# Linear attention into a PReLU feed-forward block on one core: new order of the first loads, whole output tiles in the second stage, and block 1 starting its own first output tile

## The chip, the cores and the metric

The kernel runs on one core of a Trainium2 chip. The metric is the device time of one execution in microseconds (us), lower is better. The kernels that are compared in one table row ran on the same chip as the executions of the kernel before that they are set against. "Span" is the time between the first and the last instruction that the profile shows; the device time is about 2.1 us longer.

## The reference, cut to what matters

```python
def _attn_ref(q, k, v, g_norm):                     # q, k, v: (8 batches, 8 heads, 576, 64)
    kv = np.einsum('bhsd,bhse->bhde', k, v)
    out = np.einsum('bhsd,bhde->bhse', q, kv)
    rms = np.sqrt(np.mean(out * out, axis=-1, keepdims=True) + 1e-06)
    return out / rms * g_norm

def _moe_ref(x, w_in, w_out, alpha):                # x: (4608, 512), w_in: (512, 2048), w_out: (2048, 512)
    h = x @ w_in
    g = np.maximum(h, 0.0) + alpha * np.minimum(h, 0.0)
    return g @ w_out
```

The attention output of all heads of a token is one row of x.

## The kernel before

The 4608 tokens are worked off in nine blocks of 512. In a block, 16 groups of 128 columns of h are made (four matmuls each), ScalarE takes the negative part (`m_sb`), VectorE combines both parts to `gt`, and four output tiles of 128 tokens need 16 matmuls each on `gt` and w_out. In the steady part TensorE alternates four matmuls of block w with four output matmuls of block w-1. The first two batches get their attention on TensorE in transposed form; later batches have rows that are transposed by DMA (`xm`).

The parts that the change touches:

```python
    for h0 in (0, HH):                       # batch 0, by half of the heads
        for nm in "qkv":
            load(0, nm, h0, h0 + HH)
    # ...
    def load_rest():
        for i in range(WQ):
            load_w_in(i)
        for nm in "kvq":
            zero_rest(stages[1][nm])
        load(1, "k")
        load_w_out(0)
        load(1, "q")
        load(1, "v")
        for i in range(1, WQ):
            load_w_out(i)
    # ... second stage: output matmuls of block 0 around the attention of batch 1
    LATER = 4
    def ahead(g0, g1, tiles=range(TPW)):
        for g in range(g0, g1):
            for a in tiles:
                if a < TPW - 1 or g < LATER:     # the fourth tile stops after group 4
                    y_mm(ys[a], 0, a, g)
    regroup(1, "k")
    ahead(0, 3)
    regroup(1, "q")
    step_t(1, 0, S_POOL)
    # ... three more step_t
    ahead(3, 4, range(2))
    step_kv(1, pool=S_POOL)
    # ...
    step_tail_ssq(0, S_POOL)                 # tail of batch 1: sum, Ln, Exp and norm
    ahead(15, NF)
    # ... blocks 1 to 8
    for w in range(1, NW):
        steps = phase_steps(w + 1)           # attention of the next batch, in steps
        for g in range(NF):
            a, part = divmod(g, TPW)
            parts = range(part * TPW, (part + 1) * TPW)
            if w == 1:                       # block 1: rest of block 0's fourth tile
                a, y = TPW - 1, ys[TPW - 1]
                parts = [LATER + g] if LATER + g < NF else []
            # ... begin of the step, m1_group(w, g), mid of the step,
            # y_mm for parts, end of the step
```

## Time and profile before

| | before |
|---|---|
| device time, median of 3 | 294.23 us (294.08 to 294.52) |
| span of the profiled run | 291.3 us (its device time: 293.46 us) |
| TensorE busy | 281.1 us, 96% of the span |
| TensorE's holes between the first output matmul and block 2, by starts | 1.29 us in the second stage, 1.23 us in block 1 (0.98 in the prediction) |

VectorE's timeline in block 1 of the kernel before (start, duration, instruction):

```profile
61.93 0.74 DVE L487 SCALAR_TENSOR_TENSOR gt<-m_sb,beta_sb,h_ps 128x512 f16<-128x512 f32 x1
...
63.19 0.74 DVE L487 SCALAR_TENSOR_TENSOR gt<-m_sb,beta_sb,h_ps 128x512 f16<-128x512 f32 x1
```

These are gt 7 and gt 8, 2.9 and 3.1 us behind their groups' matmuls. No output matmul waited for them, since block 1 then multiplied only gt of block 0.

The prediction says that this lag cost nothing. It overlooked a hole that the timeline hides in a merged line:

```profile
64.13 3.86 PE L478 MATMUL h_ps<-xt,w_in_sb 128*128 128x512 f16 x16
```

Sixteen matmuls 0.216 us apart, the last shown as 0.38 us, would take 3.62 us and not 3.86. The single records have the gap: 64.78 + 0.22 to 65.24, 0.25 us, ahead of group 13, and name VectorE's gt as what was waited for. Group 13 takes the bank of group 9 (the code gives banks out in fours), and gt 9 ended at 65.18.

### The profile page before, as it was taken

What the parts mean: (1) busy time and instruction counts of PE and PEld (TensorE: products, weight loads), DVE (VectorE), ACT (ScalarE), POOL (GpSimd) and SP (SyncE); (2) the same over time, 40 slices, a digit from 0 to 9 for tenths busy, and PEclk for the clock granted to TensorE, in tenths of its full rate; (3) what the DMA queues carried; (4) which work ended last, traced back from release to release, by engine and by line L of the source; (5) the groups of instructions that cost most, each with busy time, mean ns of one, the idle gap of its engine ahead of it and who ended that gap; (6) DMA issues with size and microseconds to landing.
All of it is one profiled execution on the core that took longest, in us unless ns stands there. A gap on an engine that the chain in (4) does not pass through costs nothing.

```text
span 291.3 us, 4287 instructions
## 1 busy us (share of the span) xinstructions
PE 281.1 (96%) x1551; PEld 137.8 (47%) x1551; DVE 168.8 (58%) x261; ACT 152.7 (52%) x297; POOL 100.2 (34%) x111
## 2 busy tenths in 40 slices
PE   5999999999999999999999999999999999999994
PEld 2454454544454454454445544554445444444443
DVE  4569847787667576448744764488448644444300
ACT  1459457584666565438644754476448544444210
POOL 8833410584448128424733373233003100000000
PEclk9999999999999999999999999999999999999999
DMA  7999999999899826991699189934212311222133
GB/s 89 182 206 203 200 206 198 196 202 175 134 155 184 167 42 94 204 203 30 104 206 208 34 125 184 187 49 90 46 36 56 81 36 41 47 47 47 39 72 72
DMA packets 66228, 35.54 MB, mean 122 GB/s; under 512 B 32784, under 2 KB 61728, under 8 KB 66208
## 3 DMA queue, kind: packets, MB, share of 16 engines
q0 software_dynamic: 29664, 18.35, 45.5%
q1 hardware_dynamic: 36384, 16.80, 28.3%
q8 instruction: 12, 0.20, 0.3%
q10 hardware_dynamic: 160, 0.13, 0.2%
q14 instruction: 8, 0.07, 0.1%
HBM read 36.71 MB, written 9.44 MB: 158 GB/s over the span
## 4 chain that ended last, share of the span: by engine, by line
PE 76%; DMA 17%; DVE 2%; POOL 2%; issue 1%; ACT 1%; POOLq 0%; DVEq 0%
PE y_ps L505 38%; PE h_ps L478 34%; DMA vst<-in_v_dram 7%; DMA w_in_sb<-in_moe_w_in_dram 5%; DMA w_out_sb<-in_moe_w_out_dram 4%; PE kv_ps L245 2%; PE otm_ps L397 2%; DVE gt L487 1%; DMA xm<-xrow 1%; POOL w_in_sb L165 1%; DVE xrow L430 1%; DVE ss L409 0%; POOL rg L421 0%; POOL qst L97 0%; POOL kst L97 0%
## 5 line engine op out<-in xcount | busy, mean ns | idle before, releaser
L487 DVE SCALAR_TENSOR_TENSOR gt<-m_sb,beta_sb,h_ps 128x512 f16<-128x512 f32 x144 | 105.6, 744 | 74.6 <-ACT m_sb L485 73.9
L485 ACT ACTIVATE m_sb<-h_ps 128x512 f32<-128x512 f32 x144 | 85.4, 597 | 87.3 <-PE h_ps L478 86.1
L505 PE MATMUL y_ps<-w_out_sb,gt 128*128 128x512 f16 (+1 forms) x528 | 128.8, 373 | 0.0
L478 PE MATMUL h_ps<-xm,w_in_sb 128*128 128x512 f16 x448 | 115.0, 379 | 0.2 <-DMA xm<-xrow 0.2
L505 PEld LDWEIGHTS <-gt 128*128 128x128 f16 x592 | 57.6, 98 | 64.6
L478 PEld LDWEIGHTS <-w_in_sb 128*128 128x128 f16 x584 | 55.7, 98 | 61.5 <-issue 1.7
L421 POOL TENSOR_TENSOR rg<-ss,g_all 128x512 f32<-128x512 f32 (+1 forms) x30 | 31.3, 1042 | 78.9 <-ACT ss L419 70.9
L478 PE MATMUL h_ps<-xt,w_in_sb 128*128 128x512 f16 (+1 forms) x136 | 30.6, 366 | 0.1
L515 ACT COPY y_sb<-y_ps 128x512 f32<-128x512 f32 (+1 forms) x32 | 18.4, 575 | 15.9 <-PE y_ps L505 15.9
L409 DVE TENSOR_REDUCE ss<-sqm_sb 128x8 f32<-128x512 f32 (+1 forms) x30 | 20.5, 683 | 10.5 <-ACT sqm_sb L403 10.5
L430 DVE TENSOR_TENSOR xrow<-otm_ps,rg 128x512 f16<-128x512 f32 (+1 forms) x30 | 20.5, 682 | 3.6 <-POOL rg L421 3.6
L403 ACT ACTIVATE sqm_sb<-otm_ps 128x512 f32<-128x512 f32 (+1 forms) x30 | 17.7, 591 | 6.3 <-PE otm_ps L397 6.3
L112 POOL COPY ksb<-kst 128x2560 f16<-128x2560 f16 x6 | 13.9, 2324 | 14.6 <-DMA kst<-in_k_dram 14.6
L112 POOL COPY qsb<-qst 128x2560 f16<-128x2560 f16 x5 | 11.6, 2316 | 10.0 <-issue 10.0
L397 PEld LDWEIGHTS <-qtm 128*128 128x128 f16 x120 | 9.2, 98 | 7.1 <-DMA qtm<-qsb 0.3
L204 PE MATMUL warm_ps<-warm,mask 128*128 128x512 f16 x25 | 8.5, 479 | 3.3 <-DVE eps_t L146 3.3
L397 PE MATMUL otm_ps<-kv_sb,qtm 128*128 128x128 f16 x120 | 11.6, 219 | 0.0
L245 PEld LDWEIGHTS <-ksb 128*128 128x128 f16 x160 | 9.4, 98 | 3.8 <-issue 1.5
L245 PE MATMUL kv_ps<-vst,ksb 128*128 128x128 f16 x160 | 10.4, 219 | 0.9 <-DMA vst<-in_v_dram 0.7
L416 ACT ACTIVATE ss<-ss,eps_t 128x8 f32<-128x8 f32 (+1 forms) x30 | 9.0, 301 | 3.2 <-DVE ss L409 2.9
L513 DVE COPY y_sb<-y_ps 128x256 f32<-128x256 f32 x1 | 0.4, 425 | 13.4 <-PE y_ps L505 13.4
L249 DVE TENSOR_TENSOR kv_sb<-kv_ps,mask 128x512 f16<-128x512 f32 (+1 forms) x9 | 5.6, 627 | 3.7 <-PE kv_ps L245 3.7
(76 smaller groups left out, 136.0 us busy)
## 6 DMA issues: line engine op xcount, KB each, us to landing
out_dram<-y_sb SPq DMA_DIRECT2D x70, 128.0 KB, 2.3
kst<-in_k_dram POOLq DMA_DIRECT2D x7, 320.0 KB, 8.5
qst<-in_q_dram POOLq DMA_DIRECT2D x7, 320.0 KB, 4.8
vst<-in_v_dram POOLq DMA_DIRECT2D x7, 320.0 KB, 10.6
w_in_sb<-in_moe_w_in_dram POOLq DMA_DIRECT2D x4, 512.0 KB, 10.2
w_out_sb<-in_moe_w_out_dram POOLq DMA_DIRECT2D x4, 512.0 KB, 15.0
kst<-in_k_dram POOLq DMA_DIRECT2D x7, 256.0 KB, 9.5
qst<-in_q_dram POOLq DMA_DIRECT2D x7, 256.0 KB, 6.6
```

Source lines behind the costliest of these rows:

```text
L112: (eng or nc.vector).tensor_copy(out=bufs[b % NBUF][nm][:, :, h0:h1, :].rearrange("p t h d -> p h t d"), in_=stages[b % NBUF][nm][:, h0:h1],)
L245: nc.tensor.matmul(out=kv_ps[:, j - j0, :], lhsT=ks(t), rhs=vs(t), start=(t == 0), stop=(t == NT - 1),)
L397: nc.tensor.matmul(out=ot_ps[:, 2 * j : 2 * j + 2, :], lhsT=qtms[b][:, t * NPAIR + j, :], rhs=kvs[b, j], start=True, stop=True,)
L403: nc.scalar.activation(out=sq[0:n], in_=ot_ps[0:n], func=AF.Square)
L409: nc.vector.tensor_reduce(out=ss[0:n], in_=sq[0:n], op=ALU.add, axis=mybir.AxisListType.X,)
L421: nc.gpsimd.tensor_tensor(out=rg[0:n], in0=ss[0:n].unsqueeze(2).to_broadcast([n, H, D]), in1=g_all[0:n].unsqueeze(1).to_broadcast([n, H, D ...
L430: nc.vector.tensor_mul(out=x[0:n], in0=ot_ps[0:n], in1=rg[0:n])
L478: nc.tensor.matmul(out=h_ps[:, cols], lhsT=w_in_blk(c, g), rhs=xt_of(w, c)[:, cols], start=(c == 0), stop=(c == NC - 1 and cols.stop == W),)
L485: nc.scalar.activation(out=m_sb[:], in_=h_ps[:], func=AF.Relu, scale=-1.0)
L487: nc.vector.scalar_tensor_tensor(out=gt[:], in0=m_sb[:], scalar=beta_sb[:, g : g + 1], in1=h_ps[:], op0=ALU.mult, op1=ALU.add,)
L505: nc.tensor.matmul(out=y[:], lhsT=gts[w, g][:, a * P : (a + 1) * P], rhs=w_out_blk(g)[:, cols], start=(g == 0), stop=(g == NF - 1),)
L515: nc.scalar.copy(out=y_sb[:, cols], in_=y[:])
```

## The change

The intent: (1) load q of batch 0 whole and first, so that all its transposes are out of the way while k and v land; (2) load half of w_out ahead of batch 1, so that more output matmuls can fill the time until q, k and v of batch 1 are there; (3) finish all four output tiles of block 0 in the second stage; (4) let block 1 begin its own first output tile, two groups behind the making of gt.

```diff
+    load(0, "q")
     for h0 in (0, HH):
-        for nm in "qkv":
+        for nm in "kv":
             load(0, nm, h0, h0 + HH)
@@ load_rest
-        load(1, "k")
         load_w_out(0)
-        load(1, "q")
-        load(1, "v")
-        for i in range(1, WQ):
+        load_w_out(1)
+        for nm in "kqv":
+            load(1, nm)
+        for i in range(2, WQ):
             load_w_out(i)
@@ opening: order on TensorE (cut: transposes of all heads first, fewer warm-up
@@ matmuls, two matmuls with w_in ahead of the sum of squares, groups 4 and 5 begun early)
@@ second stage (cut)
     ahead(0, 3)
     regroup(1, "q")
+    ahead(3, 6)
     step_t(1, 0, S_POOL)
...
-    step_ot(1, 0, O1)
-    step_ot(1, 1, H_POOL[0])
+    step_ot(1, 0, H_POOL[0])
+    step_ot(1, 1, O1)
...
+    ahead(10, 11)
+    step_ot(1, 3, H_POOL[0])
     norm(1, 1)
     ssq_mm(1, 2, S_POOL)
-    ahead(9, 12)
+    ahead(11, QW)
+    ahead(QW, NF, (0,))
     ssq_mm(1, 3, S_POOL)
...
@@ blocks
+    AHEAD = NF - 2
...
             if w == 1:
-                a, y = TPW - 1, ys[TPW - 1]
-                parts = [LATER + g] if LATER + g < NF else []
+                parts = [(0, g - NF + AHEAD)] if g >= NF - AHEAD else []
+            else:
+                n0 = AHEAD if w == 2 else 0
+                n1 = TPW * NF - n0
+                parts = [divmod(n0 + i, NF) for i in range(n1 * g // NF, n1 * (g + 1) // NF)]
...
+            if (w, g) == (1, 1):
+                step_tail_ssq(0, (ps_o, "o0"))
+            if (w, g) == (1, 3):
+                tail_norm(0)
             for f in end:
                 f()
```

The buffers of batch 1 are now zeroed at the start, and the norm of the tail is a function of its own, called after group 3 of block 1, just ahead of the end of that step, in which kv of batch 2 is made.

More of the change, by code (lines that the diff above doesn't have):

```diff
@@ L123, in regroup_batch @@
             regroup(b, nm, eng=nc.gpsimd)
-    for nm in "qkv":
-        zero_rest(stages[0][nm])
+    for st in stages:
+        for nm in "qkv":
+            zero_rest(st[nm])
     ident = const_p.tile([P, P], FP32, name="ident")
@@ L130 @@
     HH = H // 2
+    load(0, "q")
     for h0 in (0, HH):
-        for nm in "qkv":
+        for nm in "kv":
             load(0, nm, h0, h0 + HH)
@@ L189, in load_rest @@
             load_w_in(i)
-        for nm in "kvq":
-            zero_rest(stages[1][nm])
-        load(1, "k")
         load_w_out(0)
-        load(1, "q")
-        load(1, "v")
-        for i in range(1, WQ):
+        load_w_out(1)
+        for nm in "kqv":
+            load(1, nm)
+        for i in range(2, WQ):
             load_w_out(i)
@@ L366, in step_tail_ssq, with tail_norm @@
         nc.scalar.activation(out=rstd[:], in_=rstd[:], func=AF.Exp, bias=0.0, scale=-0.5)
+        ots["tail", i] = (ot_ps, rstd)
+    def tail_norm(i):
+        ot_ps, rstd = ots.pop(("tail", i))
         nc.vector.scalar_tensor_tensor(
@@ L385, in transpose_q @@
         )
-    n_tile = [1]
+    n_tile = [2]
     def next_o():
@@ L540 @@
     keep_warm(10)
-    regroup(0, "q", 0, HH)
     nc.vector.tensor_scalar(
@@ L544 @@
     )
+    regroup(0, "q", 0, HH)
+    regroup(0, "q", HH, H)
     step_t(0, 0, H_POOL[0])
@@ L547 @@
     regroup(0, "k", 0, HH)
-    load_rest()
-    keep_warm(8)
-    step_kv(0, 0, 2)
-    keep_warm(2)
-    step_ot(0, 0)
-    step_ot(0, 1)
-    keep_warm(1)
-    regroup(0, "q", HH, H)
-    ssq_mm(0, 0)
     step_t(0, 2, H_POOL[2])
-    step_t(0, 3, H_POOL[0])
+    step_t(0, 3, (ps_o, "o0"), nc.scalar)
     alpha_ps = ps_h.tile([P, NF], FP32, name="alpha_ps", tag="h1")
@@ L568 @@
     )
-    ssq_mm(0, 1)
+    spread_g()
+    load_rest()
+    keep_warm(4)
+    step_kv(0, 0, 2)
+    keep_warm(2)
+    step_ot(0, 0)
+    step_ot(0, 1)
     regroup(0, "k", HH, H)
-    spread_g()
+    keep_warm(2)
+    ssq_mm(0, 0)
+    ssq_mm(0, 1, H_POOL[2])
+    step_kv(0, 2, 4)
     norm(0, 0)
-    keep_warm(2)
-    step_kv(0, 2, 4)
-    keep_warm(2)
+    keep_warm(3)
     load_batch(2)
@@ L581 @@
     first += [ps_o.tile([P, W], FP32, name="h_ps", tag=f"o{g}") for g in range(2)]
+    m1_mm(first[0], 0, 0, (0,))
+    m1_mm(first[1], 0, 1, (0,))
     half_ssq(0, O2)
+    m1_mm(first[2], 0, 2, (0,))
+    m1_mm(first[3], 0, 3, (0,))
     for g in range(4):
-        m1_mm(first[g], 0, g, (0,))
-    for g in range(4):
-        if g == 2:
-            half_ssq(1, O2)
         m1_mm(first[g], 0, g, (1,))
+    half_ssq(1, O2)
+    m1_mm(first[4], 0, 4, (0, 1))
     for i in range(2):
@@ L595 @@
         if i == 0:
-            m1_mm(first[4], 0, 4, (0, 1))
-    m1_mm(first[4], 0, 4, (2, 3))
-    m1_evac(first[4], 0, 4)
-    others = {5: (ps_s, "s"), 6: (ps_y, "y"), 7: O2, 11: (ps_o, "o0"), 12: (ps_o, "o1"),
+            first.append(ps_s.tile([P, W], FP32, name="h_ps", tag="s"))
+            m1_mm(first[5], 0, 5, (0, 1))
+    for g in (4, 5):
+        m1_mm(first[g], 0, g, (2, 3))
+        m1_evac(first[g], 0, g)
+    others = {6: (ps_y, "y"), 7: O2, 11: (ps_o, "o0"), 12: (ps_o, "o1"),
               13: (ps_s, "s")}
-    for g in range(5, NF):
+    for g in range(6, NF):
         m1_group(0, g, others.get(g))
-    LATER = 4
     ys = [
@@ L616, in ahead @@
             for a in tiles:
-                if a < TPW - 1 or g < LATER:
-                    y_mm(ys[a], 0, a, g)
+                y_mm(ys[a], 0, a, g)
     S_POOL = (ps_s, "s")
     O1 = (ps_o, "o1")
+    QW = NF - GW
     regroup(1, "k")
@@ L628 @@
     step_t(1, 3, H_POOL[1], nc.scalar)
-    ahead(3, 4, range(2))
+    ahead(6, 7)
     step_kv(1, pool=S_POOL)
-    ahead(3, 4, range(2, TPW))
-    step_ot(1, 0, O1)
-    step_ot(1, 1, H_POOL[0])
+    ahead(7, 8)
+    step_ot(1, 0, H_POOL[0])
+    step_ot(1, 1, O1)
     step_ot(1, 2, H_POOL[1], nc.vector)
-    ahead(4, 5)
+    ahead(8, 9)
     ssq_mm(1, 0, S_POOL)
-    ahead(5, 7)
+    ahead(9, 10)
     ssq_mm(1, 1, S_POOL)
     norm(1, 0)
-    ahead(7, 9)
-    step_ot(1, 3, O1, nc.vector)
+    ahead(10, 11)
+    step_ot(1, 3, H_POOL[0])
     norm(1, 1)
     ssq_mm(1, 2, S_POOL)
-    ahead(9, 12)
+    ahead(11, QW)
+    ahead(QW, NF, (0,))
     ssq_mm(1, 3, S_POOL)
@@ L648 @@
     transpose_q(2)
-    ahead(12, 13)
-    step_tail_ot(0, H_POOL[1])
-    ahead(13, 15)
+    y_out(ys[0], 0, 0)
+    ahead(QW, NF, (1,))
     norm(1, 3)
-    step_tail_ssq(0, S_POOL)
-    ahead(15, NF)
-    for a in range(TPW - 1):
-        y_out(ys[a], 0, a, nc.vector if a == 1 else None)
+    step_tail_ot(0, O1)
+    ahead(QW, NF, (2,))
+    y_out(ys[1], 0, 1, nc.vector)
+    y_out(ys[2], 0, 2)
+    ahead(QW, NF, (3,))
+    y_out(ys[3], 0, 3)
     LOAD_G = 6
-    n_group[0] = 0
+    n_group[0] = 1
+    AHEAD = NF - 2
     for w in range(1, NW):
@@ L667 @@
                 load_batch(w + 2)
-            a, part = divmod(g, TPW)
-            parts = range(part * TPW, (part + 1) * TPW)
             if w == 1:
-                a, y = TPW - 1, ys[TPW - 1]
-                parts = [LATER + g] if LATER + g < NF else []
+                parts = [(0, g - NF + AHEAD)] if g >= NF - AHEAD else []
[3 more added lines that the diff above has]
+                parts = [divmod(n0 + i, NF) for i in range(n1 * g // NF, n1 * (g + 1) // NF)]
             begin, mid, end = steps.pop(0) if steps else ([], [], [])
@@ L675 @@
                 f()
-            m1_group(w, g, [H_POOL[0], S_POOL, H_POOL[2], H_POOL[1]][g % 4] if w == 1 else None)
+            m1_group(w, g, [H_POOL[1], S_POOL, H_POOL[2], H_POOL[0]][g % 4] if w == 1 else None)
             for f in mid:
                 f()
-            if 0 in parts:
-                pool, tag = ((ps_y, "y"), (ps_s, "s"))[a % 2]
-                y = pool.tile([P, W], FP32, name="y_ps", tag=tag)
-            for gg in parts:
-                y_mm(y, w - 1, a, gg)
-            if NF - 1 in parts:
-                y_out(y, w - 1, a)
+            for a, gg in parts:
+                if gg == 0:
+                    pool, tag = ((ps_y, "y"), (ps_s, "s"))[a % 2]
+                    y = pool.tile([P, W], FP32, name="y_ps", tag=tag)
+                wy = w if w == 1 else w - 1
+                y_mm(y, wy, a, gg)
+                if gg == NF - 1:
+                    y_out(y, wy, a)
+            if (w, g) == (1, 1):
+                step_tail_ssq(0, (ps_o, "o0"))
+            if (w, g) == (1, 3):
+                tail_norm(0)
             for f in end:
```

## The prediction

> **What bounds the kernel now.** I read the busy table first, then busy time by stage, then TensorE's timeline. The first fence is the busy table; the second is busy time by stretch (start:end, length, then busy us and count of PE, weight loads, DVE, ACT, POOL, then clock, DMA share, GB/s). I cut the stretches where the first matmul with w_in, the first output matmul, block 1 and block 2 begin.
>
> ```profile
> PE 281.1 (96%) x1551; PEld 137.8 (47%) x1551; DVE 168.8 (58%) x261; ACT 152.7 (52%) x297; POOL 100.2 (34%) x111
> ```
>
> ```profile
> 17.43:31.86 14.43, 14.37 (x75) 7.13 (x74) 11.83 (x21) 11.27 (x19) 4.43 (x7) 1.00 1.30 203
> 31.86:48.80 16.94, 16.13 (x110) 8.31 (x109) 10.85 (x16) 9.07 (x15) 4.27 (x6) 1.00 1.33 202
> 48.80:68.22 19.42, 18.68 (x110) 9.04 (x108) 15.83 (x25) 13.80 (x30) 10.67 (x11) 1.00 1.22 192
> 68.22:287.25 219.03, 219.01 (x1184) 106.98 (x1184) 120.35 (x173) 112.49 (x226) 66.72 (x63) 1.00 0.60 103
> ```
>
> TensorE is the bound, and from 68.22 us on it has no hole (219.01 of 219.03 us). The change cannot gain there. What remains is the opening before 17.43 us, 0.81 us idle in the second stage and 0.74 us in block 1. The timeline of TensorE names the holes (start, duration, instruction, idle before it and releaser):
>
> ```profile
> 10.25 0.72 PE L245 MATMUL kv_ps<-vst,ksb 128*128 128x128 f16 x10 [0.30 <-DMA vst<-in_v_dram]
> ...
> 17.21 0.38 PE L327 MATMUL ssq_ps<-sq_sb,mask 128*128 128x512 f16 x1 [0.47 <-ACT sq_sb L267]
> ...
> 34.97 1.29 PE L221 MATMUL qt_ps<-ident,qsb 128*128 128x128 f16 x20 [0.35 <-DVE qsb L112]
> ...
> 38.88 0.80 PE L278 MATMUL ot_ps<-qt_sb,kv_sb 128*128 128x448 f16 x5 [0.33 <-DVE kv_sb L249]
> ...
> 53.71 1.28 PE L245 MATMUL kv_ps<-vst,ksb 128*128 128x128 f16 x20 [0.43 <-DMA vst<-in_v_dram]
> ...
> 68.22 1.02 PE L478 MATMUL h_ps<-xm,w_in_sb 128*128 128x512 f16 x4 [0.23 <-DMA xm<-xrow]
> ```
>
> A matmul of 512 columns is shown as 0.38 us, but the next starts 0.216 us after it; so I measure a hole from the last start plus 0.216. The second stage then loses 0.52 us (34.23+0.22 to 34.97, transposes wait for q's regroup), 0.28 (36.31+0.22 to 36.81) and 0.49 (to 38.88, kv_sb): **1.29 us**. Block 1 loses 0.58 us before kv of batch 2 (52.91+0.22 to 53.71; v had landed at 39.45+14.1) and 0.4 before block 2 (its transposed rows arrive last): **0.98 us**. That is all that reordering after 17.43 us can win, 0.8% of the time.
>
> **What the Trainium skill says.** "TensorE: Matmul & The Clock Gate", section "Wait — 56ns, not 53.3ns?", gives 215.7 ns start to start at N=512 when warm; the trace agrees (32.07, 32.29, 32.51). So a moved matmul costs 0.216 us wherever it goes. "PSUM — Partial Sum Buffer", section "PSUM: the matmul accumulator": 8 banks, and one matmul's output fits one bank. The code names exactly eight tags (h0-h2, o0-o2, s, y), each used for tiles of up to one bank. Four held by output tiles leave four to rotate, so when a bank comes free matters. "DMA: Bandwidth & Descriptors", section "Anatomy of one DMA — SWDGE (gpsimd) path", fits 2.0 us plus bytes over 436 GB/s. That would be 3.2 us for w_out's 512 KB pieces; here they take 15.0 us from issue to landing, behind one another, at about 200 GB/s. I therefore go by landing times, not by the fit.
>
> **The change part by part.**
>
> *q whole and first.* Landing times (issue plus latency) before: half q 5.7 us, half k 7.6, half v 10.1, second halves 11.6, 13.1, 14.7, first w_in 17.2, second 19.7. The order becomes q, q, k, v, k, v. The same number of bytes precede the end of v and w_in, so these still land at 14.7 and 17.2; the first half of v moves to about 11.4. DVE also zeroes three more buffers first (3 x 0.27 = 0.8 us), so the warm-up matmuls start near 4.0, not 3.25; q's wait hides that. kv of heads' first half moves from 10.25 to about 11.6, and ACT's Square, Ln, Exp chain, which ended at 15.56, to about 16.8. The Square of the other half then begins at 16.8 instead of 16.57, in time for 17.4. TensorE meanwhile puts two matmuls on w_in ahead of that sum of squares, hiding the 0.47 us, but w_in lands only at 17.2, so they begin where the sum began. Following both orders on, the first four groups finish at 22.4 us in either. The early rate is 162 GB/s against 206 later; fewer, larger q loads may lift it a little. I allow **-0.2 us**, an estimate.
>
> *Half of w_out ahead of batch 1.* w_out 0 and 1 land near 28.7 and 31.3, batch 1 about 2.5 to 5 us later: k 33.9, q 36.3, v 39.1 (v ended at 36.6, followed by w_out 1 at 39.1; the same bytes). The last half of w_out and batch 2 keep their times (41.7, 44.9, 53.5).
>
> *Second stage.* 24 output matmuls (24 x 0.216 = 5.2 us) fill 31.87 to 37.05. q lands at 36.3, its regroup takes 0.83, so transposes start at 37.2: a hole of 0.15. Next kv starts near 39.25, as v lands; four matmuls (0.86) cover most of kv_sb, which took from 36.81 to 38.82, so 2.0 us with kv's own 1.1. Later, output tile 3 of attention asks for bank h0. The norm that frees it ended 42.71 when its sum of squares began at 40.16: 2.55 us. TensorE reaches that place ten matmuls later, 2.16 us: a hole of about 0.45. So 1.29 becomes 0.6: **-0.69 us**.
>
> *Four whole output tiles.* Twelve matmuls of the fourth tile move out of block 1 into the second stage; none is added: 0 us by themselves. Block 1 starts near 50.6 instead of 51.2 (48.80 + 12 x 0.216, less the tail's sum).
>
> *Block 1.* kv of batch 2 now comes near 54.7, after v's 53.5: the 0.58 goes. Transposed rows get as much extra time as work is put before them, so the 0.4 goes too: **-0.98 us**. But two new waits arise. First, the tail's Ln and Exp (0.69+0.63) now lie between ACT's second and third m_sb, and its norm (0.75 on DVE) lies just before kv_sb. ACT then gives m_sb 2 near 55.0; DVE works gt 2, gt 3, tail norm and kv_sb (0.7 each) to about 57.85. TensorE wants kv_sb at 56.9, after kv (1.12), a group (0.86) and an output matmul (0.22). In full 1.0 us; **+0.7** taken. Second, the output tile follows only two groups behind: gt must be ready 2.16 us after its group's matmuls. Around the first three tiles of batch 2 it was not: group 7's matmuls ended at 59.76 and its gt at 62.67, 2.9 us later, group 8's 3.1, group 9's 3.25. Before, this lag cost nothing because block 1 multiplied block 0's gt. At the full lag the waits sum to 1.0 to 1.3 us; **+0.8** taken. At the seam to block 2, gt 15 is also barely late: **+0.1**.
>
> **Sum:** -0.2 - 0.69 - 0.98 + 0.7 + 0.8 + 0.1 = -0.27 us; 294.23 - 0.27 = 293.96, so **294.0 us**.
>
> **The rivals.** (a) *The holes go and no new ones come.* ACT and DVE are 71% and 82% busy in block 1, so their lag might shrink once the arrival of kv is later and steadier. Then -0.2 - 0.69 - 0.98 gives 292.4. For it: the order looks tuned around these holes. Against it: gt's measured lag of 2.9 to 3.25 us. (b) *DVE and ACT become the bound of block 1.* Both new waits in full (1.0 + 1.3), and no gain in the opening: 294.23 - 0.69 - 0.98 + 2.3 + 0.1 = 295.0. For it: DVE's in-order queue with tail norm ahead of kv_sb. (c) *Transfers cap the second stage.* Loads already run without a gap at about 200 GB/s until 53 us. If q of batch 1 lands 1 us later than 36.3, all of it shows, since the 24 matmuls end at 37.05: about 295.0. Against it: the bytes ahead of it are known. (d) *The opening gains more.* If whole-q loads ran at 206 GB/s from the start, w_in would land some 0.5 us earlier and half a microsecond more would be saved.
>
> **Range and chances.** Rivals (a) and (b) span 292.4 to 295.0; I widen a little for rivals (c) and (d) and rounding of landing times: 292.4 to 295.4. A 2% change is 5.9 us. All post-opening holes sum to 2.3 us, so faster by 2% would need most of the opening's filler to vanish: 0.02. Slower by 2% needs a serialisation I have not seen: 0.02. Within 2%: 0.96.
>
> **What would show it right or wrong.** In the changed profile: first matmuls with w_in at about 17.2 us, and the step from h to output matmuls still near 31.9; transposes of batch 1 near 37.2 with a wait on q's regroup below 0.5 us; no DMA wait before kv of batch 2; a wait of the first otm_ps matmuls on kv_sb near 57 us; waits of output matmuls on gt in the second half of block 1; a stretch from block 2 on as dense as now. I am wrong if w_in lands clearly before 17 us (then faster), if gt keeps within 2.16 us of its group (then about 292.5), or if batch 1 arrives later than the output matmuls cover (then slower).

## More of the kernel before

The chain of work that ended last, by engine, on the page of the kernel before:

```profile
PE 76%; DMA 17%; DVE 2%; POOL 2%; issue 1%; ACT 1%; POOLq 0%; DVEq 0%
```

The 17% of DMA are, but for 1% of transposed rows, the loads of the first 54 us, one queue that from 4 us on moves 162 to 214 GB/s; the chain leaves it at the last load of batch 2's v.

## The result, and the profile after

The changed kernel takes 293.40 us (median of 4, 293.03 to 293.72) against 294.15 us (median of 4). The ratio is 0.9973 with a 95% interval of 0.9955 to 0.999: the same within 2%, and a small gain. Ratios in this text are from fast runs of the same rounds; they are not quite the ratio of the medians. They agree with the ratio of the means of all listed executions within 0.0002, but for two kernels whose first, profiled execution stands apart: whole q alone (0.9974, 0.9981 by all five) and loads as before (1.0149 and 1.0136). A second timing, on another chip, gives 0.9979 (0.9958 to 0.9999). There three of the kernel before's 11 executions took 295.0 to 295.5 us and lift its mean; by medians the gain is only 0.3 us (293.65 against 293.96).

The profile after: the busy table's first line and, below it, the chain of work that ended last.

```profile
PE 280.4 (96%) x1547; PEld 137.0 (47%) x1547; DVE 167.5 (57%) x258; ACT 153.6 (53%) x299; POOL 99.1 (34%) x109
...
PE 88%; ACT 3%; DVE 3%; DMA 2%; issue 1%; POOL 1%; DVEq 0%; POOLq 0%
```

The DMA queue has left the chain (17% to 2%): TensorE and the waits on ScalarE and VectorE carry it from the opening on.

Busy time by stretch (columns as in the prediction), cut at the same four places of the program as in the prediction (first matmul with w_in, first output matmul, block 1, block 2):

```profile
16.50:31.53 15.03, 14.77 (x74) 7.16 (x75) 12.78 (x21) 11.91 (x21) 4.22 (x6) 1.00 1.27 204
31.53:50.14 18.61, 18.40 (x121) 9.46 (x120) 10.60 (x16) 9.78 (x17) 4.78 (x7) 1.00 1.36 201
50.14:70.89 20.75, 19.52 (x113) 9.21 (x111) 15.58 (x24) 13.28 (x29) 10.98 (x12) 1.00 1.18 191
70.89:287.35 216.46, 216.20 (x1171) 105.51 (x1169) 120.31 (x173) 112.72 (x226) 65.87 (x62) 1.00 0.59 102
```

TensorE's idle time fell from 0.81 to 0.21 us in the second stage and rose from 0.74 to 1.23 us in block 1. From block 2 on it is dense as before, but for 0.26 us, most of which is the seam below. TensorE's timeline says who was waited for:

```profile
16.50 0.61 PE L482 MATMUL h_ps<-xt,w_in_sb 128*128 128x512 f16 x2 [0.29 <-DMA w_in_sb<-in_moe_w_in_dram]
...
36.71 1.28 PE L221 MATMUL qt_ps<-ident,qsb 128*128 128x128 f16 x20
...
44.94 0.39 PE L278 MATMUL ot_ps<-qt_sb,kv_sb 128*128 128x64 f16 x2 [0.21 <-DVE xt L305]
...
54.24 1.28 PE L245 MATMUL kv_ps<-vst,ksb 128*128 128x128 f16 x20
...
57.23 0.38 PE L401 MATMUL otm_ps<-kv_sb,qtm 128*128 128x128 f16 x4 [0.63 <-DVE kv_sb L249]
...
63.84 0.39 PE L509 MATMUL y_ps<-w_out_sb,gt 128*128 128x512 f16 x1 [0.60 <-DVE gt L491]
...
65.09 0.39 PE L509 MATMUL y_ps<-w_out_sb,gt 128*128 128x512 f16 x1
...
72.31 0.60 PE L509 MATMUL y_ps<-w_out_sb,gt 128*128 128x512 f16 x2 [0.18 <-DVE gt L491]
```

The transposes at 36.71 and kv of batch 2 at 54.24 no longer wait. The wait for the bank of the fourth attention tile (44.94), the wait on kv_sb (57.23), and the waits on gt (63.84 and the two that follow it, and 72.31) are new. As before, holes are measured from starts: 44.35 + 0.22 to 44.94 is 0.37 us; 56.22 + 0.22 to 57.23 is 0.79; 62.21 + 0.86 to 63.84 is 0.77, and the next two output matmuls come 0.17 and 0.16 late; 71.75 + 0.22 to 72.31 is 0.34. VectorE's timeline of the changed kernel shows what the 57.23 waited for:

```profile
54.42 1.41 DVE L491 SCALAR_TENSOR_TENSOR gt<-m_sb,beta_sb,h_ps 128x512 f16<-128x512 f32 x2 [0.97 <-ACT m_sb L489]
55.74 0.74 DVE L371 SCALAR_TENSOR_TENSOR xm<-ot_ps,g2col,rstd 128x512 f16<-128x512 f32 x1
56.41 0.68 DVE L249 TENSOR_TENSOR kv_sb<-kv_ps,mask 128x512 f16<-128x512 f32 x1
```

VectorE worked in the order of the program: gt 2 and 3, the tail's norm (L371), and only then kv_sb, although kv's matmuls had ended at 55.52.

At an equal place in block 3 (the output matmuls right after kv) the two first traces stand at 103.95 us before and 103.99 us after. So by this pair of traces the change moved time but won none, while the timed runs say 0.75 us. The experiments had to explain both.

### The profile page after: what moved, and what is told of

Same layout as the page of the kernel before. It is cut to its first block, busy times and chain, and to the rows that moved or that the text cites. A ratio compares the mean times of both kernels' runs of the same rounds, so it can differ in the third digit from the quotient of the medians.

```text
span 291.4 us, 4273 instructions
## 1 busy us (share of the span) xinstructions
PE 280.4 (96%) x1547; PEld 137.0 (47%) x1547; DVE 167.5 (57%) x258; ACT 153.6 (53%) x299; POOL 99.1 (34%) x109
## 3 DMA queue, kind: packets, MB, share of 16 engines
HBM read 36.71 MB, written 9.44 MB: 158 GB/s over the span
## 4 chain that ended last, share of the span: by engine, by line
PE 88%; ACT 3%; DVE 3%; DMA 2%; issue 1%; POOL 1%; DVEq 0%; POOLq 0%
PE h_ps L482 40%; PE y_ps L509 38%; PE kv_ps L245 3%; PE otm_ps L401 2%; DMA qst<-in_q_dram 2%; DVE gt L491 1%; PE yb L509 1%; PE yc L509 1%; PE ya L509 1%; PE yd L509 1%; PE qt_ps L221 1%; ACT m_sb L489 1%; ACT rstd L296 1%; PE ot_ps L278 1%; ACT rstd L299 1%
## 5 line engine op out<-in xcount | busy, mean ns | idle before, releaser
L509 PE MATMUL y_ps<-w_out_sb,gt 128*128 128x512 f16 (+1 forms) x528 | 131.3, 373 | 0.8 <-DVE gt L491 0.8
L425 POOL TENSOR_TENSOR rg<-ss,g_all 128x512 f32<-128x512 f32 (+1 forms) x30 | 31.2, 1041 | 80.5 <-ACT ss L423 75.7
L204 PE MATMUL warm_ps<-warm,mask 128*128 128x512 f16 x21 | 7.3, 489 | 4.1 <-DVE eps_t L148 4.1
L231 ACT COPY qt_sb<-qt_ps 128x576 f16<-128x576 f16 x4 | 2.4, 638 | 12.4 <-PE qt_ps L221 12.4
```

The costliest lines, as they stand in the source:

```text
L425: nc.gpsimd.tensor_tensor(out=rg[0:n], in0=ss[0:n].unsqueeze(2).to_broadcast([n, H, D]), in1=g_all[0:n].unsqueeze(1).to_broadcast([n, H, D ...
L509: nc.tensor.matmul(out=y[:], lhsT=gts[w, g][:, a * P : (a + 1) * P], rhs=w_out_blk(g)[:, cols], start=(g == 0), stop=(g == NF - 1),)
```

## The experiments

One measure serves for all traces. From the start of the first output matmul to the start of the first matmul of block 2, less 0.216 us for each output matmul in between (64 before, 78 in the changed kernel), is the time of all other work and holes of the second stage and block 1. I call it the **middle**. It leaves out the opening itself, which differs from run to run: in nine traces with the changed kernel's opening and its loads of batch 0 the first output matmul starts between 31.23 and 31.91 us. It is not free of what the opening does later: a TensorE that comes early waits longer for the same loads. In the runs with lag four and with both edits (31.26 and 31.23 us) the holes ahead of the transposes and of kv of batch 1 are 0.22 and 0.18, and 0.18 and 0.19 us; in the changed kernel's first trace (31.53) 0.00 and 0.08.

| kernel | first output matmul | first of block 2 | output matmuls between | middle | ratio to before (95%) |
|---|---|---|---|---|---|
| before, first trace | 31.86 | 68.22 | 64 | 22.5 | 1 |
| before, again | 31.70 | 68.77 | 64 | 23.2 | one look |
| before, third | 31.50 | 68.59 | 64 | 23.3 | one look |
| changed | 31.53 | 70.89 | 78 | 22.5 | 0.9973 (0.9955 to 0.999) |
| changed again | 31.76 | 71.05 | 78 | 22.4 | 0.9979 (0.9958 to 0.9999) |
| kv before the tail | 31.60 | 70.50 | 78 | 22.1 | 0.9963 (0.9941 to 0.9985) |
| lag four | 31.26 | 69.83 | 76 | 22.2 | 0.9936 (0.9916 to 0.9956) |
| both | 31.23 | 69.25 | 76 | 21.6 | 0.9920 (0.9899 to 0.9942) |
| lag one | 31.86 | 75.11 | 79 | 26.2 | 1.0111 (1.0078 to 1.0144) |
| q in halves | 32.50 | 72.08 | 78 | 22.7 | 0.9999 (0.9972 to 1.0027) |
| loads as before | 31.91 | 74.43 | 78 | 25.7 | 1.0149 (1.0111 to 1.0188) |
| lag three, kv first, bank | 31.91 | 69.55 | 77 | 21.0 | 0.9916 (0.9890 to 0.9942) |
| before, whole q alone | 32.73 | 68.84 | 64 | 22.3 | 0.9974 (0.9961 to 0.9988) |
| lag three etc., again | 31.83 | 69.36 | 77 | 20.9 | 0.9928 (0.9915 to 0.9940) |

All gave correct results. The theory was that the new waits in block 1 cost about what the removed holes had cost; the rival was that they cost nothing, since the transposed rows of batch 2 would set the start of block 2 anyway.

### The changed kernel again

No edit.

> The changed kernel once more, unaltered, to learn whether the measured 0.27% is real and to have its time beside the other runs of this chip. Theory T (the change removed about 2.1 us of TensorE holes, 0.33 in the opening, 0.77 in the second stage, 0.98 in block 1 and its end, and put about 2.2 us of new waits into block 1 and its seam): ratio to the kernel before between 0.995 and 1.000, and the same waits in the trace: first otm matmul on kv_sb 0.8 us, output matmuls 7 to 9 on gt 1.1 us together, one on gt 15 0.3 us. Rival R (the new waits cost nothing, since the transposed rows of batch 2 set the start of block 2 in any case): same time here; told apart by the other runs.

Measured: 293.65 us (median of 6), ratio 0.9979. The waits come back to the hundredth: 0.63 us on kv_sb and 0.60 us on gt 7 are what the timeline shows ahead of the same two matmuls. The new waits are real. So is a small gain, though by this set alone barely (the interval ends at 0.9999).

### kv of batch 2 ahead of the tail's norm

```diff
-            if (w, g) == (1, 3):
-                tail_norm(0)
             for f in end:
                 f()
+            if (w, g) == (1, 3):
+                tail_norm(0)
```

> Only kv of batch 2 (its product with the mask on VectorE) goes ahead of the tail's norm. Theory T: kv_sb then ends about 0.67 us earlier, the first otm matmul's wait falls from 0.8 us to about 0.1, and everything after comes 0.65 us earlier: ratio to the kernel before about 0.995 (0.0022 below the unaltered changed kernel). The waits on gt (1.1 us) stay. Rival R: the wait turns up again at the start of block 2, and the time stays as the changed kernel's, ratio 0.997.

TensorE's timeline of this run, the first otm matmul and the output matmul that waits on gt 7:

```profile
56.76 0.38 PE L401 MATMUL otm_ps<-kv_sb,qtm 128*128 128x128 f16 x4
...
63.45 0.39 PE L509 MATMUL y_ps<-w_out_sb,gt 128*128 128x512 f16 x1 [0.68 <-DVE gt L491]
```

The hole ahead of the otm matmul is 0.13 us (56.41 + 0.22 to 56.76) instead of 0.79, as expected. The wait on gt 7 stays, a little longer (0.68). Mean times of the same rounds are 293.14 against 293.65 us, 0.5 us less; the middle fell by about 0.4. The gain passes through to the end, nearly in full: the rival predicted none. The rest went into waits of 0.19 us ahead of kv of batch 1 (0.08 in the changed kernel) and of 0.84 on gt 7 by starts (0.77).

### The own output tile four groups behind

```diff
-    AHEAD = NF - 2
+    AHEAD = NF - 4
```

> Block 1's own first output tile follows four groups behind instead of two (12 of its matmuls in block 1 instead of 14, the other 2 in the next stage). Theory T: all waits of output matmuls on gt, 1.1 us in block 1 and 0.3 at its end, vanish, the wait on kv_sb (0.8) stays; 1.4 us less than the changed kernel, ratio about 0.9925. Rival R: TensorE then waits about 1.4 us at the first matmul of block 2 for its transposed rows, and the time stays, ratio 0.997.

The same timeline of this run:

```profile
57.30 0.38 PE L401 MATMUL otm_ps<-kv_sb,qtm 128*128 128x128 f16 x4 [1.07 <-DVE kv_sb L249]
...
69.83 1.03 PE L482 MATMUL h_ps<-xm,w_in_sb 128*128 128x512 f16 x4
```

No output matmul waits on gt any more, and block 2 begins without waiting for its rows. The wait on kv_sb grew from 0.63 to 1.07 us as the profile shows it (0.79 to 1.23 by starts), where I had expected it to stay: two output matmuls fewer lie ahead of it. The mean is 292.40 us, 1.25 us below the changed kernel of the same rounds; 1.4 was expected. The part that reached the end includes the 0.34 us of the seam, which lies after the middle. In the middle this trace shows only 0.3 us less (22.5 and 22.4 to 22.2): its early opening brought the waits for q and v of batch 1 named above.

### Both edits

The two diffs above together.

> Both edits. Theory T: the gains add up, 0.65 + 1.4 = 2.05 us less than the changed kernel, ratio about 0.990; transposed rows also arrive 0.65 us earlier, so block 2 does not wait for them by more than 0.3 us. Rival R: no gain, ratio 0.997, with a wait at the first matmul of block 2 of some 2 us.

TensorE's waits between 50 and 73 us in this run (engine, what it waited for, us in total, times, longest) are down to one line:

```profile
PE otm_ps L401 <- DVE kv_sb L249: 0.4, 1, 0.4
```

The mean is 291.94 us, 1.7 us below the changed kernel; the gains of the two runs above sum to 1.76. They add up, so they are separate costs on TensorE's own line, and the rival is out.

### One group behind

```diff
-    AHEAD = NF - 2
+    AHEAD = NF - 1
```

> The other direction: block 1's own first output tile follows one group behind instead of two. Theory T (an output matmul waits as long as gt of its group needs beyond the matmuls put between): one group and one output matmul give 1.08 us, and even an undisturbed gt takes 1.4 us after its group, so nearly every one of the 15 output matmuls waits 0.3 us and those of groups 7 to 9 longer; 3 to 5 us more than the changed kernel, ratio to before 1.008 to 1.015. Rival R (the lag does not matter to the time): ratio 0.998 as before.

TensorE's waits in this run hold, among others:

```profile
PE y_ps L509 <- DVE gt L491: 3.8, 9, 1.1
```

Ratio 1.0111, inside the range expected; the middle is 3.7 us longer than in the changed kernel. With one, two and four groups of lag, waits on gt by the same view are 3.8, 0.8 and 0 us. The cause of these waits is settled.

### q of batch 0 first, but in halves

```diff
-    load(0, "q")
+    load(0, "q", 0, HH)
+    load(0, "q", HH, H)
```

> The changed kernel with q of batch 0 still first, but in four loads by half of the heads instead of two whole ones. Theory S (fewer, larger loads made the opening 0.3 to 0.6 us faster): the first w_in lands again near 17.1 us instead of 16.5, the first output matmul of block 0 returns from 31.5 to about 31.85; 0.3 us slower than the changed kernel. Rival O (the order, or the zeroing moved ahead, did it): w_in at 16.5 and the output matmul at 31.5 as in the changed kernel.

Busy time by stretch from 6 to 9 us, of three kernels. Only the last column is of interest, what the DMA engines moved in GB/s. First the kernel before, then the changed kernel, then this run:

```profile
6.00:9.00 3.00, 3.00 (x19) 1.51 (x18) 1.44 (x5) 0.64 (x1) 2.99 (x5) 1.00 1.28 166
```

```profile
6.00:9.00 3.00, 2.84 (x16) 1.15 (x15) 0.94 (x3) 0.00 (x0) 2.13 (x5) 1.00 1.39 193
```

```profile
6.00:9.00 3.00, 3.00 (x13) 1.44 (x12) 0.29 (x1) 0.00 (x0) 2.37 (x4) 1.00 1.20 153
```

The same bytes in the same order, cut in four loads instead of two, move at 153 instead of 193 GB/s in these three microseconds. The first w_in lands at 17.8 us (issued at 10.35, 7.4 us later) instead of 16.5 (8.99 + 7.5), and the first output matmul starts at 32.50, outside the range of the nine traces of the changed kernel's opening. The time goes back to the kernel before's: ratio 0.9999, mean 294.28 us. For the rate the size of the loads decides, and not the order: all ten traces with whole q, that of whole q alone below among them, have 191 to 197 GB/s in this stretch, and the four with halves 153 to 172. What the rate is worth in time is less sure. This trace fell on the slowest of six executions (294.70 us; the median is 294.21), so w_in 1.3 us later than in the first trace of the changed kernel, in place of 0.6, is an upper example (in the nine traces w_in lands at 15.9 to 17.0 us). The two intervals (0.9999 here, 0.9979 for the changed kernel on another chip) overlap, so the time alone does not carry the verdict.

### The changed kernel with the loads ordered as before

```diff
-        load_w_out(0)
-        load_w_out(1)
-        for nm in "kqv":
-            load(1, nm)
-        for i in range(2, WQ):
+        load(1, "k")
+        load_w_out(0)
+        load(1, "q")
+        load(1, "v")
+        for i in range(1, WQ):
             load_w_out(i)
```

> The changed kernel with the order of loads of the kernel before (k of batch 1, w_out 0, q, v, w_out 1 to 3). Theory T (half of w_out ahead and 24 output matmuls ahead of the transposes belong together): the matmuls with the second piece of w_out come up at 35.0 us and wait until it lands near 39.1, so 4 us are lost, ratio about 1.012. Rival (the second stage is not bound by which load comes first): below 1 us lost, ratio below 1.001.

TensorE's timeline:

```profile
38.61 0.38 PE L509 MATMUL ya<-w_out_sb,gt 128*128 128x512 f16 x1 [3.09 <-DMA w_out_sb<-in_moe_w_out_dram]
```

The second piece of w_out comes at 38.6 us. Ratio 1.0149; by the means of all executions 4.0 us slower than before (298.34 against 294.33), where the changed kernel is 0.3 to 0.8 quicker, so rather more than the 4 us expected. The trace fell on the quickest of five executions (296.88 us), so it shows less than the mean; the other four also had a lower granted clock (0.991 to 0.992, here 0.996), and how much of their 298.3 to 298.9 us is the clock stays open. The output matmuls that part 3 puts ahead of the transposes need part 2's early w_out. The reverse, an early w_out without them, was not run.

### A version with three edits

Lag three, kv ahead of the tail's norm, and:

```diff
-    ahead(10, 11)
+    ahead(10, QW)
     step_ot(1, 3, H_POOL[0])
     norm(1, 1)
     ssq_mm(1, 2, S_POOL)
-    ahead(11, QW)
     ahead(QW, NF, (0,))
```

> A version to beat both: kv ahead of the tail's norm, the own output tile three groups behind, and the output matmuls of group 11 put ahead of the fourth attention tile, which waits 0.2 to 0.4 us for its bank. Theory T: 3.24 us of lag covers gt's 2.9 to 3.25, so its waits stay below 0.2 us together; the wait for the bank goes (0.37); kv_sb's wait falls to about 0.2. That is 0.3 to 0.5 us below the version with both edits and lag four: ratio about 0.9905. Rival: the bank's wait moves to the sum of squares of the fourth tile, or the transposed rows of batch 2 are waited for at block 2; then ratio 0.992 again.

The fourth attention tile no longer waits for its bank: it starts at 45.73 us, 0.216 after the matmul ahead of it. But the wait only moved on, as the rival had it, to a sum of squares a few matmuls later:

```profile
46.16 1.03 PE L509 MATMUL ya<-w_out_sb,gt 128*128 128x512 f16 x4
47.38 0.38 PE L294 MATMUL ssq_ps<-sq_sb,mask 128*128 128x512 f16 x1 [0.18 <-ACT rstd L296]
```

By starts that is 0.35 us (46.81, where the fourth of these matmuls starts, + 0.22 to 47.38) in place of 0.38 at the bank. The waits on gt are down to 0.06 us in this trace, and that on kv_sb is 0.35 (0.57 with both edits). The middle is 21.0, 0.6 below that of both edits; 0.37 of it are the waits for q and v of batch 1 that the earlier opening there (31.23 us, here 31.91) brought. The mean, 291.82 us, is about theirs (291.94, on another chip); the ratio, 0.9916, is the rival's 0.992, and its interval also holds theory T's 0.9905. That this version beats both edits is not shown.

### The kernel before, a second and a third look

No edit, twice.

> The kernel before once more, for a second profile: the start of the first output matmul moved between 31.23 and 31.91 us in eight profiles with the changed kernel's opening, and the one profile of the kernel before has 31.86. Theory P (the timed gain of 0.2 to 0.3% is the opening, and the first profile of before fell on a quick opening): 32.0 to 32.6 us here, span 291.6 or more, and from that matmul to the first of block 2 again 36.4 us. Rival Q (the opening is no faster): 31.2 to 31.9 us.

> The kernel before a third time, for the spread of its opening: Theory P: first output matmul again later than 31.9 us; Rival Q: within 31.2 to 31.9 us.

Theory P falls in its wording: the first output matmul starts at 31.70 and 31.50 us, no later than in the changed kernel, and the stretch to block 2 is 37.1 us in both, not 36.4. The spans, 291.9 and 291.7 us, are as P expected, but for another reason: the middle is 23.2 and 23.3 instead of the first trace's 22.5. By starts the holes sum to 3.23 and 3.25 us against 2.53, and what differs most are waits on DMA. The wait ahead of block 2 was 0.23 us in the first trace; in the third, TensorE's timeline has:

```profile
53.56 1.28 PE L245 MATMUL kv_ps<-vst,ksb 128*128 128x128 f16 x20 [0.60 <-DMA vst<-in_v_dram]
...
68.59 1.02 PE L478 MATMUL h_ps<-xm,w_in_sb 128*128 128x512 f16 x4 [0.75 <-DMA xm<-xrow]
```

So in both later looks the kernel before loses 0.7 us more between the same points than in the trace that I predicted from.

### Whole q alone, in the kernel before

```diff
+    load(0, "q")
     for h0 in (0, HH):
-        for nm in "qkv":
+        for nm in "kv":
             load(0, nm, h0, h0 + HH)
```

> The kernel before with one part of the change alone: q of batch 0 whole and first, all else as before. Theory P (whole q makes the loads of the opening end earlier): first w_in about 0.4 us earlier than in the kernel before, first output matmul at 31.2 to 31.9 us, ratio about 0.998. Rival Q: the first heads' kv comes about 1.2 us later and nothing is won at the end of the opening; ratio 1.000 to 1.003.

By time, this one part gives 0.9974 (0.9981 with its slowest, profiled execution), about as much as the whole change (0.9973 and 0.9979). In its trace the rate from 6 to 9 us is 192 GB/s, as in the changed kernel, and w_in lands at 16.6 us (16.9 to 17.2 in three traces of before), but the last load of batch 2 at 53.5, no earlier than before. But theory P's other number is a miss: the first output matmul is at 32.73 us, not 31.2 to 31.9, since TensorE waits 1.24 us for the first q. The profiled execution was the slowest of five (294.07 us; the others 293.16 to 293.43), so the trace doesn't show where a typical run of it wins. It does show that most of that lost microsecond is made up by block 2 (68.84 against 68.22 to 68.77): the waits on v vanish, as TensorE arrives later, though that for the rows of block 2 grows to 1.01 us by starts.

### The version with three edits again

> The version with three edits (kv ahead of the tail's norm, lag three, group 11 ahead of the fourth attention tile) a second time, beside other runs of before: ratio 0.990 to 0.993; from the first output matmul to the first of block 2, less 0.216 us for each further output matmul in between, 34.8 us again, against 36.4 before.

TensorE's waits between 31 and 73 us:

```profile
PE otm_ps L401 <- DVE kv_sb L249: 0.2, 1, 0.2
PE ssq_ps L294 <- ACT rstd L296: 0.2, 1, 0.2
```

291.92 us (median of 5), ratio 0.9928 (0.9915 to 0.9940), middle 20.9. It beats both kernels: 2.1 us below before (means 291.91 and 294.00), and some 1.7 us below the changed kernel (mean 293.65, on another chip). That is what both edits alone gave; the second line is the wait that moved on.

## Why the prediction was right

The forecast was 294.0 us, the same within 2%, with -0.27 us as the sum of gains and new waits. Measured were 293.4 and 293.65 us, which is -0.3 to -0.8 us, by medians and means of the two timings. The range held, and the sum was small for the reason given: gains of about 2 us paid back by new waits of about as much. That it came so near is in part luck, since errors in the terms cancel. Step by step:

- **Opening, -0.2 predicted.** The sign fits; the size stays open. What was mis-sized is the load rate: "may lift it a little". From 6 to 9 us whole loads move 191 to 197 GB/s where halves move 163 to 172 (three traces of before), w_in lands at 15.9 to 17.0 us in nine traces of the new opening (predicted 17.2, with "clearly before 17 us" named as a sign of being wrong), and the last load of batch 2 at 52.5 to 52.9 us against 53.5 to 53.9. Taken back alone, the part costs the whole timed gain by the point estimate (0.9999); put in alone, it gives it (0.9974; 0.57 us by the means of all executions). The intervals overlap, so how much of the gain is the loads' is not shown. That TensorE's own opening would be no quicker was right within its scatter (31.23 to 31.91 against 31.50 to 31.86 us).
- **Second stage, -0.69 predicted.** Right: 0.52 us of holes are left of 1.29, so -0.77. The transposes have no hole at all (0.15 predicted), since q of batch 1 lands at 35.5, not 36.3; the bank's hole is 0.37 (0.45 predicted, though 2.55 less 2.16 is 0.39).
- **Block 1, -0.98 predicted.** Right for both holes named: neither kv of batch 2 nor block 2 waits. A third hole, the 0.25 us ahead of group 13, was overlooked and is gone too, so -1.23. In the two later looks at before the first two sum to 1.19 and 1.68 us.
- **Wait on kv_sb, +0.7 taken of 1.0.** Right: 0.79 us, for the reason named, and 0.13 once kv goes ahead of the norm.
- **Waits on gt 7 to 9, +0.8 taken of 1.0 to 1.3.** Somewhat low: 0.77 + 0.17 + 0.16 = 1.10 us. gt 7 came 2.7 us after its group (63.78 less 61.08), near the 2.9 measured before the change. I ought to have taken both waits in full. That the lag had cost nothing before was wrong by those 0.25 us.
- **Seam, +0.1 predicted.** Too low: 0.34 us.

Against the first trace of before the pieces are -0.33 (opening, this pair of traces), -0.77, -1.23, +0.79, +1.10 and +0.34, together -0.10 us; the traces differ by +0.04 at block 3. The gap between that and the timed gain is about the 0.7 us by which the first trace's middle is shorter than in the two later looks. What stays open: whether the timed gain comes from the holes that the new order closed or from the quicker loads, which shorten the same waits on DMA; why halves of a load move slower than wholes in the first microseconds; and how whole q alone gains its 0.57 us in a typical execution, since its only trace fell on its slowest run.

Of the rivals, (a) (no new waits) failed, since 2.2 us of them came; (b) (ScalarE and VectorE become the bound in block 1) was the nearest for that stage, with new waits of 1.89 us there of its 2.3, and (d) (the opening gains more) for the loads; (c) did not occur.

## What to carry to other kernels

When work is moved forward to fill a hole, ask for each moved instruction what it now reads and how late that is in the engine that makes it: an output that no output matmul waited for may be almost 3 us behind, and a consumer two steps behind will pay for it. In an in-order queue, put what the bound engine waits for ahead of what can wait: swapping two VectorE instructions was worth 0.5 us. When a wait is gone, look where it went: the bank's 0.38 us came back as 0.35 us ahead of a sum of squares. And take more than one trace before crediting a hole of half a microsecond; the first trace of a kernel may be its quickest execution.

## What the Trainium skill lacked or had wrong

- "TensorE: Matmul & The Clock Gate", section "Back-to-back issue gap", gives about 131 ns per matmul as sustained at N=512 in a stream with weight loads, and says the isolated formula (216 ns) over-counts. Here such a stream keeps 216 ns from start to start (36.06, 36.28, 36.50 us in the changed kernel, each with its own weight load), as the same page's section "Wait — 56ns, not 53.3ns?" has it.
- "DMA: Bandwidth & Descriptors", section "Anatomy of one DMA — SWDGE (gpsimd) path": the fit of 2.0 us plus bytes over 436 GB/s does not give the landing time in a queue that is kept full. The 512 KB pieces of w_out took a median of 15.0 us from issue to landing, at some 200 GB/s in the kernel before.
- Pages advise larger loads in general, but I found none that says what cutting a load costs in a queue that already holds the next ones. Here q of batch 0 in halves of the heads, with the same runs, moved at 153 GB/s against 193 whole, from 6 to 9 us; what that is worth in time is not settled by these runs (ratios 0.9999 and 0.9979, with intervals that overlap).
